# Window attention into a gated feed-forward layer on one core: masks in six steps, one inversion for both heads, an untied exponential, and earlier weights

## The chip, the core and the metric

The kernel runs on one core of a Trainium2 chip. The core has five engines that work through queues of their own, each in order: TensorE (PE; its weight loads are shown apart as PEld), VectorE (DVE), ScalarE (ACT), GpSimd (POOL) and SyncE (SP), which here only issues transfers; 16 DMA engines carry those out. The metric is the device time of one execution in microseconds (us). The kernel before takes 1011.78 us, the median of three runs (1010.85 to 1012.56).

## The reference

Eight batches of eight heads (head size 64) attend over 576 positions, each position to itself and the 63 before it. The result, 4608 tokens of 512 numbers, goes through a gated feed-forward layer. Everything is in 32-bit floats in and out.

```python
scores = scale * np.matmul(q, k.transpose(0, 1, 3, 2))
mask = (rel >= 0) & (rel < window)
scores = np.where(mask, scores, -1000000000.0)
scores = scores - np.max(scores, axis=-1, keepdims=True)
attn = np.exp(scores)
attn = attn / (np.sum(attn, axis=-1, keepdims=True) + 1e-09)
out = np.matmul(attn, v)
...
gate = 1.0 / (1.0 + np.exp(-(x @ w_gate)))
val = x @ w_val
return (gate * val @ w_out).astype(np.float32)
```

## The kernel before

**Tiling.** The 4608 tokens are 12 tiles of 384 (t, in an order of their own). The eight heads are four pairs (p = 0 to 3), so a tile has four units of attention, written (t,p). In a unit the 384 tokens are six blocks of 64, and a block attends to 128 keys (its own and the block before). The hidden layer's 1536 columns are 12 blocks of 128 (j); each j has three weight matrices, m = 0 (gate), 1 (value) and 2 (output). The number of a weight piece is i = 3j + m, so i = 3 and 4 are gate and value of the second block, i = 2 and 5 the output weights of the first and second.

**One unit of attention.** TensorE makes the scores of both heads (`s0`, `s1`, L208). VectorE adds the mask, scales, and takes the row minimum of the negated scores (L230, three per head). ScalarE takes the exponentials (L239, three per head); the row sums of head 0 come with them, those of head 1 of tiles 0 and 1 from a VectorE reduction (L248). VectorE adds 1e-9 and inverts (L249, L250), and GpSimd multiplies the rows by the inverses (L252). TensorE transposes (`pp`, L283), ScalarE copies the result out (`pT`, L288), TensorE multiplies by v (`oo`, L312), and ScalarE and VectorE split the result into a high and a low part (`x`, L318 and L319).

**The front.** All eight units of tiles 0 and 1 come first. Each step has a due time in a list of events: unit n = 4t + p has its scores at A0 + 3.6n, its softmax, transposes and products at fixed distances behind. The events are sorted by due time; that is the order in which the code issues them. TensorE keeps that order. On the other engines a scheduler orders the instructions by its own estimate, within the dependencies and the bindings that the code gives with `tc.issue_after(x)`: an instruction issued within it comes behind x. In the front the exponentials of unit n are bound behind the transposed copies of unit n - 2.

**The weights.** Each weight piece arrives as 64-bit words (`raw`, six buffers) and is turned into 32-bit floats: ScalarE makes two conversions (`w32` L111, `raw` L112; three `w32` buffers), VectorE three bit operations (`zz` L120, then L122, L124), ScalarE the rounded high part (L145) and VectorE the low part (L146). For m < 2 the float form is stored (`w32d`, L139), and parts of the split form too (`wd`, L447), for the tiles that come later. A `w32` buffer is free again when its store has landed. `conv_a`, `conv_b` and `conv_c` are bound behind marks: in the front those of i = 3 behind the split of unit (1,2), those of i = 2, 4 and 5 behind that of (1,3).

**Tiles 0 and 1, then pairs of tiles.** The hidden blocks of tiles 0 and 1 follow: for each j the gate product (`ph0`, 12 matmuls of 384 columns, L342), the value product (`ph1`), and, one block behind, the output product (`y`, nine matmuls of 512 columns, L407). The `ph` products go round three PSUM banks. The gate's sigmoid (`g`, L363) is ScalarE's, and needs another function table than the exponentials (an ACT_TABLE_LOAD at each change). From tile 2 on the tiles go in pairs with seven products in place of eight (`pr`, L537), and the attention of the next pair is spread between them.

**The masks.** Three 128x128 masks are made before all else: one for inner blocks, two for the first block of a sequence, one for each head. GpSimd sets each to zero and cuts it with selections on 64 rows.

Of the code, what the change and the prediction touch: the masks (L58 to L72), `softmax`, `exponentials`, `normalize` and `stage_n` (L212 to L276), the table of due times (L608 to L612) and the marks of the conversions (L732 to L748).

## Time and profile before

| what | us |
|---|---|
| median of three runs | 1011.78 |
| the profiled execution, its own time | 1013.32 |
| its span, first to last instruction | 1011.5 |
| TensorE busy in the span | 981.8 (97%) |
| VectorE busy | 675.8 (67%) |
| ScalarE busy | 527.2 (52%) |
| GpSimd busy | 236.1 (23%) |

A share is a mean over the whole span. The front and the stretch of the conversions, the first 100 us or so, load the engines otherwise than the rest. A TensorE that is shown busy may be waiting inside a matmul, since ends of matmuls are modelled; the number of matmuls in a stretch says more. The granted clock is given as a share of 2.4 GHz.

### The profile page before, as it was taken

What the parts mean: (1) busy time and instruction counts of PE and PEld (TensorE: products, weight loads), DVE (VectorE), ACT (ScalarE), POOL (GpSimd) and SP (SyncE); (2) the same over time, 40 slices, a digit from 0 to 9 for tenths busy, and PEclk for the clock granted to TensorE, in tenths of its full rate; (3) what the DMA queues carried; (4) which work ended last, traced back from release to release, by engine and by line L of the source; (5) the groups of instructions that cost most, each with busy time, mean ns of one, the idle gap of its engine ahead of it and who ended that gap; (6) DMA issues with size and microseconds to landing.
All of it is one profiled execution on the core that took longest, in us unless ns stands there. A gap on an engine that the chain in (4) does not pass through costs nothing.

```text
span 1011.5 us, 19901 instructions
## 1 busy us (share of the span) xinstructions
PE 981.8 (97%) x6984; PEld 884.0 (87%) x6984; DVE 675.8 (67%) x1846; ACT 527.2 (52%) x1465; POOL 236.1 (23%) x251
## 2 busy tenths in 40 slices
PE   5899999998999999999999999999999999999998
PEld 4798998887899978999988999988999998999996
DVE  6789889757887874766675766675666677344542
ACT  7878886744654644545554654554555454211122
POOL 5200117254540030212131221213211124010100
PEclk9999999999999999999999999999999999999999
DMA  9899988899997624767652776760776662466500
GB/s 299 297 348 367 342 288 278 277 333 342 320 324 267 216 85 152 232 220 221 202 172 70 240 234 200 222 204 32 228 232 219 207 192 74 146 219 204 192 32 32
DMA packets 115924, 221.52 MB, mean 219 GB/s; under 512 B 9456, under 2 KB 61936, under 8 KB 115824
## 3 DMA queue, kind: packets, MB, share of 16 engines
q1 hardware_dynamic: 115824, 220.24, 65.9%
q8 instruction: 56, 0.92, 0.4%
q14 instruction: 44, 0.36, 0.1%
HBM read 178.52 MB, written 41.68 MB: 218 GB/s over the span
## 4 chain that ended last, share of the span: by engine, by line
PE 73%; DVE 7%; ACT 7%; DMA 6%; issue 3%; POOL 1%; SPq 0%; DVEq 0%; ACTq 0%; POOLq 0%
PE pr L537 36%; PE y L407 24%; PE ph L342 6%; ACT p L239 3%; PE pp L283 2%; PE s L208 2%; DMA wd<-w 2%; DMA wd<-ws 2%; ACT g L352 1%; ACT e L351 1%; PE oo L312 1%; PE s L312 1%; DMA wt<-wd 1%; DVE u L543 1%; DVE p L230 1%
## 5 line engine op out<-in xcount | busy, mean ns | idle before, releaser
L537 PE MATMUL pr<-x_T,wt 128*128 128x384 f32 x1440 | 284.6, 339 | 4.7 <-DVE u L543 3.6
L537 PEld LDWEIGHTS pr<-x_T,wt 128*128 128x128 f32 x1440 | 252.6, 188 | 20.1 <-DVE u L543 11.2
L407 PE MATMUL y<-w,hh 128*128 128x512 f32 x804 | 250.2, 392 | 0.0
L537 PE MATMUL pr<-x_B,wt 128*128 128x384 f32 x1080 | 222.2, 342 | 4.7 <-ACT xf L267 4.0
L537 PEld LDWEIGHTS pr<-x_B,wt 128*128 128x128 f32 x1080 | 188.7, 189 | 15.6 <-ACT xf L267 4.3
L407 PEld LDWEIGHTS y<-w,hh 128*128 128x128 f32 x804 | 148.3, 188 | 21.3 <-ACT hh L372 1.3
L543 DVE TENSOR_TENSOR u<-pr,p 128x384 f32<-128x384 f32 x120 | 66.6, 555 | 143.3 <-PE pr L537 143.0
L407 PE MATMUL y<-w,hl 128*128 128x512 f32 x402 | 158.6, 394 | 0.5 <-DVE hl L376 0.4
L252 POOL TENSOR_TENSOR p<-p,rs 128x384 f32<-128x384 f32 x76 | 65.0, 860 | 278.2 <-DVE rs L250 227.5
L239 ACT ACTIVATE p<-p,mn 128x128 f32<-128x128 f32 x288 | 111.1, 394 | 23.6 <-DVE mn L230 22.7
L376 POOL TENSOR_TENSOR hl<-h,hh 128x384 fp32r<-128x384 f32 x48 | 49.8, 1038 | 296.2 <-DVE hh L374 296.2
L342 PE MATMUL ph<-x,w 128*128 128x384 f32 x576 | 109.2, 343 | 1.8 <-DVE w L146 1.3
L342 PEld LDWEIGHTS ph<-x,w 128*128 128x128 f32 x576 | 100.9, 190 | 5.4 <-DVE w L146 1.6
L407 PEld LDWEIGHTS y<-w,hl 128*128 128x128 f32 x402 | 75.3, 187 | 19.3 <-DVE hl L376 3.1
L230 DVE CUSTOM_DVE_ANT_0 p<-s,m 128x128 f32<-128x128 f32 x288 | 66.4, 285 | 15.7 <-PE s L208 8.5
L543 DVE TENSOR_TENSOR c<-pr,u 128x384 f32<-128x384 f32 x120 | 66.6, 555 | 7.8 <-ACT g L568 3.3
L376 DVE TENSOR_TENSOR hl<-hb,hh 128x384 fp32r<-128x384 f32 x60 | 39.1, 663 | 40.9 <-ACT hh L372 40.5
L351 ACT ACTIVATE e<-c 128x384 f32<-128x384 f32 x72 | 37.4, 522 | 52.6 <-DVE c L543 51.6
L548 ACT COPY p<-pr 128x384 f32<-128x384 f32 x60 | 28.2, 470 | 70.4 <-PE pr L537 69.8
L288 ACT COPY pT<-pp 128x384 f32<-128x384 f32 x96 | 41.2, 481 | 41.6 <-PE pp L283 41.6
L356 DVE SCALAR_TENSOR_TENSOR g<-g,e 128x384 f32<-128x384 f32 x96 | 55.2, 589 | 5.7 <-ACT e L353 5.6
L354 DVE TENSOR_SCALAR g<-g 128x384 int32<-128x384 int32 x96 | 40.2, 425 | 25.9 <-ACT g L352 25.9
(84 smaller groups left out, 1238.7 us busy)
## 6 DMA issues: line engine op xcount, KB each, us to landing
wt<-wd SPq DMA_DIRECT2D x210, 512.0 KB, 4.2
v<-in_vN_dram SPq DMA_DIRECT2D x48, 384.0 KB, 4.9
wd<-ws SPq DMA_DIRECT2D x48, 256.0 KB, 5.3
k<-in_kT_dram SPq DMA_DIRECT2D x48, 224.0 KB, 5.0
q<-in_qT_dram SPq DMA_DIRECT2D x48, 192.0 KB, 4.7
wd<-w SPq DMA_DIRECT2D x36, 256.0 KB, 6.0
out_dram<-yo SPq DMA_DIRECT2D x33, 256.0 KB, 2.0
raw<-in_moe_w_gate_dram SPq DMA_DIRECT2D x12, 512.0 KB, 5.9
```

What stands on the lines that cost most here:

```text
L230: nc.vector.tensor_tensor_reduce(out=pt[:, u, :], in0=sc[:, u, :], in1=masks[key], op0=ALU.add, op1=ALU.min, scale=-SCALE, scalar=3.0e38, ...
L239: exp = nc.scalar.activation(pt[:, u, :], pt[:, u, :], AF.Exp, bias=mn[:, u:u + 1], scale=-1.0, **sums)
L252: eng.tensor_mul(out=pt, in0=pt, in1=rs.unsqueeze(2).broadcast_to([P, UP, P]))
L288: cp = nc.scalar.copy(pT, pp)
L342: pe(nc.tensor.matmul(ph, l, r, start=i == 0, stop=i == len(prs) - 1))
L351: nc.scalar.activation(e, ph, AF.Relu, scale=-1.0)
L354: nc.vector.tensor_scalar(out=g.bitcast(I32), in0=g.bitcast(I32), scalar1=0x7FFFFFFF, scalar2=None, op0=ALU.bitwise_and)
L356: nc.vector.scalar_tensor_tensor(out=g, in0=g, scalar=1.0, in1=e, op0=ALU.add, op1=ALU.mult)
L376: return eng.tensor_sub(out=h_lo, in0=h32, in1=h_hi.bitcast(F32))
L407: pe(nc.tensor.matmul(yb[y], l, r, start=first and n == 0, stop=last and n == 2))
L537: pe(nc.tensor.matmul(ps, l, r, start=new and i == 0, stop=i == len(prs) - 1, skip_group_check=not new))
L543: nc.vector.tensor_add(out=o, in0=ps, in1=a)
```

## The change

It has four parts.

1. The inner mask is set to zero by VectorE and cut by GpSimd in four selections. The two other masks are VectorE copies of it, each cut once more on 64 rows. This stands ahead of the identity matrix; before, the identity and three memsets came first or between, and fourteen selections made the masks.
2. The row sums of both heads of a unit lie in one tile (`rs`, 128x6). One addition and one inversion serve both, and the two multiplications follow. `normalize` now takes a whole unit, in all 12 tiles.
3. The exponentials of unit (1,3) are not bound behind the transposed copies of (1,1). The due times of the transposes and products of units (1,2) and (1,3) move forward: 9.2 and 10.4 for n = 6 in place of 10.6 and 12.2, 7.3 in place of 8.4 for the transposes of n = 7.
4. The conversions of i = 3 follow the split of unit (1,1), those of i = 4 that of (1,2).

```diff
+    masks = {key: const.tile([P, P], F32, name=f"m_{key[0]}{key[1]}") for key in ((0, 0), (1, 0), (0, 1))}
+    band = masks[0, 0]
+    nc.vector.memset(band, 0.0)
+    for h in range(2):
+        rows = band[h * BLK:(h + 1) * BLK]
...
+    for h, key in enumerate(((1, 0), (0, 1))):
+        nc.vector.tensor_copy(out=masks[key], in_=band)
+        rows = masks[key][h * BLK:(h + 1) * BLK]
+        nc.gpsimd.affine_select(out=rows, in_=rows, pattern=[[1, P]], compare_op=ALU.is_ge,
+                                fill=NEG, base=-BLK, channel_multiplier=0)
     ident = const.tile([P, P], F32, name="ident")
     make_identity(nc, ident)
...
             exponentials(t, p, h, sc[h])
-            normalize(t, p, h)
+        normalize(t, p)
...
-        rs = sm.tile([P, UP], F32, name=f"rs{h}_{t}_{p}", tag="rs")
+        if h == 0:
+            rs_of[(t, p)] = sm.tile([P, 2, UP], F32, name=f"rs_{t}_{p}", tag="rs")
+        rs = rs_of[(t, p)][:, h, :]
...
-                if NP * t + p - 2 in marks["pT"]:
+                if NP * t + p - 2 in marks["pT"] and (t, p) != (1, NP - 1):
...
-    def normalize(t, p, h):
-        pt, rs = st[(t, p, h)]
-        if t < 2 and h:
-            nc.vector.reduce_sum(out=rs, in_=pt, axis=mybir.AxisListType.X)
+    def normalize(t, p):
+        rs = rs_of.pop((t, p))
+        if t < 2:
+            nc.vector.reduce_sum(out=rs[:, 1, :], in_=st[(t, p, 1)], axis=mybir.AxisListType.X)
         nc.vector.tensor_scalar_add(out=rs, in0=rs, scalar1=1e-9)
         nc.vector.reciprocal(out=rs, in_=rs)
         eng = nc.vector if t == 3 and p % 2 or t // 2 == 2 else nc.gpsimd
-        eng.tensor_mul(out=pt, in0=pt, in1=rs.unsqueeze(2).broadcast_to([P, UP, P]))
-        st[(t, p, h)] = pt
+        for h in range(2):
+            pt = st[(t, p, h)]
+            eng.tensor_mul(out=pt, in0=pt, in1=rs[:, h, :].unsqueeze(2).broadcast_to([P, UP, P]))
...
-                        (0, 3.5 if n > 1 else 0, 10.6 - n // 7 * 2.2, 12.2)):
+                        (0, 3.5 if n > 1 else 0, {6: 9.2, 7: 7.3}.get(n, 10.6), {6: 10.4}.get(n, 12.2))):
...
-                early = {3: ("1_2",), 2: ("1_3",), 4: ("1_3",), 5: ("1_3",)}.get(a[0], (key,))
+                early = {3: ("1_1",), 4: ("1_2",), 2: ("1_3",), 5: ("1_3",)}.get(a[0], (key,))
```

How the instructions stand now is shown at three places. The first is GpSimd's queue from the start of the program to its first multiplication, before (`m_00`, `m_10` and `m_01` are the masks).

```order
masks.py:197 MEMSET ident_81 128x128
L61 MEMSET m_00_86 128x128
masks.py:199 ISA
masks.py:199 AFFINE_SELECT ident_81<-ident_81 128x128
L64 AFFINE_SELECT m_00_86<-m_00_86 64x128 x2
L61 MEMSET m_10_100 128x128
L66 AFFINE_SELECT m_00_86<-m_00_86 64x128
L61 MEMSET m_01_117 128x128
...
L66 AFFINE_SELECT m_01_117<-m_01_117 64x128 x2
L69 AFFINE_SELECT m_10_100<-m_10_100 64x128
L69 AFFINE_SELECT m_01_117<-m_01_117 64x128
L252 TENSOR_TENSOR p0_0_0_266<-p0_0_0_266,rs0_0_0_268 128x384
```

And the same place in the changed kernel.

```order
L61 ISA
L61 AFFINE_SELECT m_00_81<-m_00_81 64x128 x2
masks.py:197 MEMSET ident_105 128x128
L63 AFFINE_SELECT m_00_81<-m_00_81 64x128 x2
masks.py:199 AFFINE_SELECT ident_105<-ident_105 128x128
L68 AFFINE_SELECT m_10_82<-m_10_82 64x128
L68 AFFINE_SELECT m_01_83<-m_01_83 64x128
L256 TENSOR_TENSOR p0_0_0_242<-p0_0_0_242,rs_0_0_244 128x384
L256 TENSOR_TENSOR p1_0_0_251<-p1_0_0_251,rs_0_0_244 128x384
```

Fourteen selections on masks have become six, and the three memsets have gone; the scheduler has put the identity's two instructions between them. The two multiplications of a unit now take one `rs` tile.

The second place is ScalarE's queue at the end of the front, before (`p0_1_3` is head 0 of unit (1,3), `x_1_1` the split of unit (1,1), `g_0_0` the first gate of tile 0, `w32_0_1` the conversion of i = 3).

```order
L239 ACTIVATE p1_1_2_668<-p1_1_2_668,mn1_1_2_669 128x128 x3
L318 CAST x_1_0_708<-oo_1_0_695 128x384
L288 COPY pT0_1_1_715<-pp0_1_1_711 128x384
L288 COPY pT1_1_1_721<-pp1_1_1_717 128x384
L239 ACTIVATE p0_1_3_723,rs0_1_3_725<-p0_1_3_723,mn0_1_3_724 128x128 x3
L239 ACTIVATE p1_1_3_735<-p1_1_3_735,mn1_1_3_736 128x128 x3
L318 CAST x_1_1_761<-oo_1_1_748 128x384
L363 ACT_TABLE_LOAD
L363 ACTIVATE g_0_0_777<-ph0_0_0_764 128x384
...
L318 CAST x_1_2_835<-oo_1_2_822 128x384
L111 ACTIVATE w32_0_1_838<-raw_0_1_330 128x512
```

And in the changed kernel.

```order
L241 ACTIVATE p1_1_2_623<-p1_1_2_623,mn1_1_2_624 128x128 x3
L241 ACTIVATE p0_1_3_678,rs_1_3_680<-p0_1_3_678,mn0_1_3_679 128x128 x3
L241 ACTIVATE p1_1_3_687<-p1_1_3_687,mn1_1_3_688 128x128 x3
L317 CAST x_1_0_663<-oo_1_0_650 128x384
L287 COPY pT0_1_1_670<-pp0_1_1_666 128x384
L287 COPY pT1_1_1_676<-pp1_1_1_672 128x384
L317 CAST x_1_1_713<-oo_1_1_700 128x384
L111 ACTIVATE w32_0_1_790<-raw_0_1_300 128x512
...
L145 CAST w0_1_797<-w32_0_1_790 128x2x256
L362 ACT_TABLE_LOAD
L362 ACTIVATE g_0_0_741<-ph0_0_0_728 128x384
```

The exponentials of (1,3) have gone ahead of the split of (1,0), and the whole conversion of the second block's gate weights stands ahead of the table load. On TensorE the transposes of (1,2) have gone ahead of the first gate product, the products of (1,2) and the transposes of (1,3) ahead of the first value product.

The third place is ScalarE's queue around `g_1_0`, the first gate of tile 1, before (`w32_0_2` and `w32_1_2` are conversions of the third block).

```order
L363 ACTIVATE g_1_0_880<-ph0_1_0_867 128x384
L145 CAST w0_1_845<-w32_0_1_838 128x2x256
L145 CAST w1_1_940<-w32_1_1_907 128x2x256
L112 ACTIVATE raw_0_2_882<-raw_0_2_882 128x512
L112 ACTIVATE raw_1_2_884<-raw_1_2_884 128x512
L145 CAST w2_0_950<-w32_2_0_912 128x512
L111 ACTIVATE w32_0_2_972<-raw_0_2_882 128x512
L111 ACTIVATE w32_1_2_977<-raw_1_2_884 128x512
```

And in the changed kernel.

```order
L317 CAST x_1_3_816<-oo_1_3_803 128x384
L111 ACTIVATE w32_2_0_864<-raw_2_0_389 128x512
L112 ACTIVATE raw_2_0_389<-raw_2_0_389 128x512
L111 ACTIVATE w32_0_2_924<-raw_0_2_834 128x512
L112 ACTIVATE raw_2_1_862<-raw_2_1_862 128x512
L111 ACTIVATE w32_1_2_929<-raw_1_2_836 128x512
L362 ACTIVATE g_1_0_832<-ph0_1_0_819 128x384
L145 CAST w2_0_902<-w32_2_0_864 128x512
```

`g_1_0` stood ahead of the third block's conversions and stands behind two of them now. From the tenth block on the queues of all engines are alike but for the normalization.

## Rows read from the trace of the kernel before

**Rows 1.** The page: the span, the busy time of TensorE, and the shares of the chain that ended last.

```profile
span 1011.5 us, 19901 instructions
PE 981.8 (97%) x6984; PEld 884.0 (87%) x6984; DVE 675.8 (67%) x1846; ACT 527.2 (52%) x1465; POOL 236.1 (23%) x251
PE 73%; DVE 7%; ACT 7%; DMA 6%; issue 3%; POOL 1%; SPq 0%; DVEq 0%; ACTq 0%; POOLq 0%
```

**Rows 2.** The windows view: stretch in us, its length, busy time (and instructions) of PE, PEld, DVE, ACT and POOL, the granted clock, the DMA engines' busy share, and GB/s.

```profile
25.00:30.00 5.00, 2.79 (x38) 1.77 (x32) 4.96 (x34) 5.00 (x20) 2.10 (x3) 1.00 1.05 388
40.00:45.00 5.00, 4.84 (x69) 4.25 (x67) 3.67 (x8) 4.20 (x10) 0.00 (x0) 1.00 0.41 129
45.00:50.00 5.00, 3.41 (x17) 2.77 (x17) 4.94 (x10) 4.71 (x10) 0.00 (x0) 1.00 0.92 250
50.00:55.00 5.00, 5.00 (x20) 5.00 (x21) 3.52 (x8) 3.13 (x6) 0.00 (x0) 0.66 0.86 216
80.00:100.00 20.00, 18.71 (x154) 16.53 (x154) 18.98 (x48) 17.09 (x37) 2.26 (x2) 1.00 1.03 376
100.00:120.00 20.00, 20.00 (x157) 18.70 (x150) 17.08 (x57) 16.56 (x40) 1.82 (x2) 1.00 0.95 346
```

**Rows 3.** The timeline of the start: start in us, length, engine, line and operation, and in brackets the idle time before it and what ended that. The first scores, GpSimd's last mask selections, the first mask addition, the first exponential.

```profile
3.91 1.56 PE L208 MATMUL s<-k,q 64*64 64x128 f32 x24 [3.91 <-DMA k<-in_kT_dram]
1.35 0.64 POOL L64 TENSOR_SCALAR_AFFINE_SELECT m<-m 64x128 f32<-64x128 f32 x2
5.97 0.64 POOL L69 TENSOR_SCALAR_AFFINE_SELECT m<-m 64x128 f32<-64x128 f32 x2
6.29 0.29 DVE L230 CUSTOM_DVE_ANT_0 p<-s,m 128x128 f32<-128x128 f32 x1 [5.43 <-POOL m L69]
6.62 0.40 ACT L239 ACTIVATE p<-p,mn 128x128 f32<-128x128 f32 x1 [4.40 <-DVE mn L230]
```

**Rows 4.** The timeline of VectorE and GpSimd around 26 to 29 us: head 1's inversion of unit (1,0), an addition that runs beside a multiplication, and then GpSimd's multiplications of (1,0) head 1 and (1,1) head 0.

```profile
26.74 0.17 DVE L250 RECIPROCAL rs<-rs 128x3 f32<-128x3 f32 x1
27.27 0.66 DVE L249 TENSOR_SCALAR rs<-rs 128x3 f32<-128x3 f32 x1
27.08 0.82 POOL L252 TENSOR_TENSOR p<-p,rs 128x384 f32<-128x384 f32 x1 [1.63 <-DVE rs L250]
28.28 0.83 POOL L252 TENSOR_TENSOR p<-p,rs 128x384 f32<-128x384 f32 x1 [0.38 <-DVE rs L250]
```

**Rows 5.** The timeline of ScalarE from the copies of (1,0) to the gate's table load, and the first conversions and high parts of the second block.

```profile
28.23 0.86 ACT L288 COPY pT<-pp 128x384 f32<-128x384 f32 x2
30.14 0.99 ACT L239 ACTIVATE p<-p,mn 128x128 f32<-128x128 f32 x3
32.96 0.48 ACT L318 CAST x<-oo 128x384 fp32r<-128x384 f32 x1 [1.83 <-PE oo L312]
33.84 0.86 ACT L288 COPY pT<-pp 128x384 f32<-128x384 f32 x2 [0.40 <-PE pp L283]
34.58 0.41 ACT L239 ACTIVATE p<-p,mn 128x128 f32<-128x128 f32 x1
36.63 0.46 ACT L318 CAST x<-oo 128x384 fp32r<-128x384 f32 x1
38.04 1.28 ACT L363 ACT_TABLE_LOAD   x1 [0.95 <-PE ph L342]
39.34 0.49 ACT L363 ACTIVATE g<-ph 128x384 f32<-128x384 f32 x1
42.63 0.67 ACT L111 ACTIVATE w<-raw 128x512 f32<-128x512 f32 x1
43.20 0.67 ACT L112 ACTIVATE raw<-raw 128x512 int32<-128x512 uint32 x1
47.29 0.64 ACT L145 CAST w<-w 128x512 fp32r<-128x512 f32 x1
```

**Rows 6.** The timeline of TensorE from the first gate product to the first output product.

```profile
35.59 2.37 PE L342 MATMUL ph<-x,w 128*128 128x384 f32 x12
45.01 2.70 PE L342 MATMUL ph<-x,w 128*128 128x384 f32 x14 [0.17 <-DVE x L319]
47.98 0.62 PE L342 MATMUL ph<-x,w 128*128 128x384 f32 x2 [0.27 <-ACT w L145]
49.91 5.66 PE L342 MATMUL ph<-x,w 128*128 128x384 f32 x22 [1.31 <-DVE w L146]
55.41 0.63 PE L407 MATMUL y<-w,hh 128*128 128x512 f32 x2
```

**Rows 7.** The timeline again: a conversion's steps on VectorE (`zz`, L122, L124), a ScalarE conversion that waits for a store, and one scores product later on. Then, from the view of the transfers between 40 and 100 us, the stores of the float weights: issues, KB each, us to landing.

```profile
43.33 0.43 DVE L120 TENSOR_SCALAR zz<-w 128x512 int32<-128x512 int32 x1
43.80 0.69 DVE L122 SCALAR_TENSOR_TENSOR w<-w,zz 128x512 int32<-128x512 int32 x1
44.87 0.68 DVE L124 CUSTOM_DVE_ANT_0 w<-raw,w 128x1024 uint16<-128x1024 uint16 x1
52.91 1.24 ACT L111 ACTIVATE w<-raw 128x512 f32<-128x512 f32 x2 [1.87 <-DMA w32d<-w]
80.95 0.88 PE L208 MATMUL s<-k,q 64*64 64x128 f32 x22 [1.07 <-ACT xf L300]
...
w32d<-w SPq DMA_DIRECT2D x11, 256.0 KB, 5.3
```

More of the change, by code (lines that the diff above doesn't have):

```diff
@@ L53, in attn_ffn @@
     ps_a = ctx.enter_context(tc.tile_pool(name="ps_a", bufs=2, space=PSUM))
+    masks = {key: const.tile([P, P], F32, name=f"m_{key[0]}{key[1]}") for key in ((0, 0), (1, 0), (0, 1))}
[4 more added lines that the diff above has]
+        nc.gpsimd.affine_select(out=rows, in_=rows, pattern=[[1, P]], compare_op=ALU.is_ge,
+                                fill=NEG, base=-1, channel_multiplier=-1)
+        nc.gpsimd.affine_select(out=rows, in_=rows, pattern=[[-1, P]], compare_op=ALU.is_ge,
+                                fill=NEG, base=BLK, channel_multiplier=1)
+    for h, key in enumerate(((1, 0), (0, 1))):
+        nc.vector.tensor_copy(out=masks[key], in_=band)
+        rows = masks[key][h * BLK:(h + 1) * BLK]
+        nc.gpsimd.affine_select(out=rows, in_=rows, pattern=[[1, P]], compare_op=ALU.is_ge,
+                                fill=NEG, base=-BLK, channel_multiplier=0)
     ident = const.tile([P, P], F32, name="ident")
     make_identity(nc, ident)
-    masks = {}
-    for key in ((0, 0), (1, 0), (0, 1)):
-        m = const.tile([P, P], F32, name=f"m_{key[0]}{key[1]}")
-        nc.gpsimd.memset(m, 0.0)
-        for h in range(2):
-            rows = slice(h * BLK, (h + 1) * BLK)
-            nc.gpsimd.affine_select(out=m[rows], in_=m[rows], pattern=[[1, P]], compare_op=ALU.is_ge,
-                                    fill=NEG, base=-1, channel_multiplier=-1)
-            nc.gpsimd.affine_select(out=m[rows], in_=m[rows], pattern=[[-1, P]], compare_op=ALU.is_ge,
-                                    fill=NEG, base=BLK, channel_multiplier=1)
-            if key[h]:
-                nc.gpsimd.affine_select(out=m[rows], in_=m[rows], pattern=[[1, P]], compare_op=ALU.is_ge,
-                                        fill=NEG, base=-BLK, channel_multiplier=0)
-        masks[key] = m
     warm = const.tile([P, 1], F32, name="warm")
@@ L153, in attn_ffn @@
     xs, xf = {}, {}
-    ld, vts, st, kk, sc_of = {}, {}, {}, {}, {}
+    ld, vts, st, kk, sc_of, rs_of = {}, {}, {}, {}, {}, {}
     def load_qk(t, p):
@@ L242, in exponentials @@
                 chain.append(exp.ins)
-        st[(t, p, h)] = pt, rs
-    def normalize(t, p, h):
-        pt, rs = st[(t, p, h)]
-        if t < 2 and h:
-            nc.vector.reduce_sum(out=rs, in_=pt, axis=mybir.AxisListType.X)
+        st[(t, p, h)] = pt
+    def normalize(t, p):
+        rs = rs_of.pop((t, p))
+        if t < 2:
+            nc.vector.reduce_sum(out=rs[:, 1, :], in_=st[(t, p, 1)], axis=mybir.AxisListType.X)
         nc.vector.tensor_scalar_add(out=rs, in0=rs, scalar1=1e-9)
@@ L272, in stage_s @@
         exponentials(t, p, 1, sc[1])
-    def stage_n(t, p):
-        for h in range(2):
-            normalize(t, p, h)
     def stage_b(t, p):
@@ L596, in attn_ffn @@
     APT = (0.9, 0.8, 0.9, 1.5, 0)
-    stages = (stage_a, stage_b, stage_c, stage_s, stage_n)
+    stages = (stage_a, stage_b, stage_c, stage_s, normalize)
     LOAD_AHEAD = 8
```

## The prediction

> **What bounds the kernel now.** I read the page first. TensorE is busy 97% of the span and has 73% of the chain that ended last [rows 1], so the other engines count only where TensorE waits. The windows view says where that is [rows 2]. From 100 us on a stretch of 20 is full: 157 matmuls in 20.00 us busy. Before that there are holes. Between 25 and 30 us TensorE is busy 2.79 of 5 while ScalarE has 5.00 and VectorE 4.96: the front belongs to these two. Between 45 and 50 it runs 17 instructions where 5 us have room for 27 matmuls of the size seen below. Between 50 and 55 its granted clock is 0.66 on the mean, so it ran part of that stretch at 1.2 GHz instead of 2.4.
>
> The timelines then give the reasons. At the start the first mask addition waits for GpSimd's last masks, not for the scores [rows 3]. Before 45 us ScalarE waits 1.83 and 0.40 us for TensorE, and the exponentials of the last unit stand behind those waits [rows 5]. At 47.98 TensorE waits 0.27 us for the second block's weights, at 49.91 again 1.31, and the 22 matmuls from there take 5.50 us to the first output product [rows 6]. I look for the gain there, since behind it TensorE goes on with little idle time.
>
> **The masks.** The last selection ends at 5.97 + 0.64 = 6.61, the first addition starts at 6.29; the scores that it also needs end at 3.91 + 1.56 = 5.47 [rows 3]. A selection costs 0.32. Six of them and two instructions for the identity, at that price each, are 2.6 us from about 0.9, so the masks are there by 4 us; VectorE's memset and two copies run beside them. The addition then waits for the scores alone and starts near 5.55: 0.7 us earlier. It can't be more, because the scores wait for k from the DMA.
>
> **One inversion for both heads.** Removed per unit: one addition and one inversion, about 0.2 us of VectorE. Something else goes too: the addition of head 0 ran beside GpSimd's multiplication of the unit before and took 0.66 instead of the 0.17 of a neighbouring inversion; it ends as GpSimd does (27.08 + 0.82) [rows 4]. In the new order the addition stands behind the reduction and some mask additions, where GpSimd is done. Against that stands a longer path: both multiplications wait for the one inversion, where head 0's ran ahead of it. Behind the inversion of (1,0) at 26.74, GpSimd ended 27.90 and the copies began at 28.23 [rows 4, 5]; now 0.83 comes on top. The start's 0.7 and some 0.4 of VectorE's go into paying for that. I take 0.25 us earlier for the exponentials of (1,2), which end at 30.75 instead of 31.0. The bounds: 0.8 earlier if the second multiplication hides behind ScalarE's other work, 0.5 later if VectorE saves nothing. In the later tiles the 48 units lose as many instructions, but TensorE is the bound there: nothing.
>
> **The untied exponentials.** Those of (1,3) need the mask additions of (1,3), which stand behind a reduction: 0.75 us behind 30.75, so 31.5, in place of 34.58 [rows 5]. They take 2.05 (34.58 to 36.63). From here ScalarE is nearly full, and I add its queue in the new order, by start-to-start times [rows 5]: the split of (1,0) 0.36 and the copies of (1,1) 0.74 end at 34.65, about where the copies ended before. The product of (1,1) takes TensorE 0.9; its split ends at 35.95 (before 37.0). The 3 us won are filled with other work, not yet a gain.
>
> **The second block's weights.** The two conversions of i = 3 come now (0.57 and 0.56, to 37.1) instead of at 42.63. Then the copies of (1,2), to 37.8. The high part, which came at 47.29, waits for three VectorE steps of 0.35, 0.6 and 0.6 [rows 7]: 38.1 to 38.6. The table load 1.28 and the gate 0.40 end at 40.3, some 0.6 later than before [rows 5]. Split of (1,2) 0.36, the conversions of i = 4 1.13, the copies of (1,3) 0.74: 42.5. The high part of i = 4 (waiting for VectorE) 43.4, two `raw` 1.12, the split of (1,3) 0.36: 44.9, and its low part on VectorE 0.47: 45.35. TensorE's 14 matmuls need that low part; they started at 45.01 [rows 6]. So up to here the kernel is 0.35 us *later*: the conversions were moved ahead of the split, and ScalarE is the queue that everything stands in.
>
> But the weights are there by 44.2. The 14 matmuls end near 47.85, and the 24 of block 1 follow at once. Twelve take 2.17 at full clock (35.59: 2.37 less the last one's overlap of 0.2), so 24 take 4.35: the first output product starts at 52.2, in place of 55.41. Gain 3.2 us. About 1.6 of it are the two waits, 1.5 the clock (22 matmuls at 0.181 are 4.0, not 5.5), and the rest small.
>
> That assumes that the clock doesn't fall. Before it fell TensorE had run two matmuls between 47.7 and 49.91 [rows 6]. In the new order I see one idle stretch of 0.9 us ahead of the products of (1,3), with work on either side. If the clock falls all the same, 1.5 us are lost again.
>
> **The sum.** The page's span is 1011.5 in an execution of 1013.32, which is 1.54 above the median of 1011.78. 1013.32 - 3.2 = 1010.1 in that execution, and 1011.78 - 3.2 = **1008.6** against the median. This takes it that 55 to 100 us, where the conversions keep VectorE (18.98 of 20) and the DMA engines (share 1.03) full [rows 2], moves forward as a whole. I think so, since the DMA engines have a hole to fill: 129 and 250 GB/s between 40 and 50 us against 376 later [rows 2], together some 1.9 MB or 5 us of transfers, and the changed order issues the second block's stores and the fourth block's loads into it.
>
> One rule speaks against moving the table load into a full stretch. In the trace the load takes 1.28 us and the gate starts 0.02 behind it [rows 5]; ahead of it stand 0.95 us idle which the view puts to TensorE. The Trainium skill's page "ScalarE: Activation LUTs", section "What ACT_TABLE_LOAD costs", counts a drain of about 1.38 us to each switch on top of the load. By that rule the forecast would be an estimate of 1010.0 us. The trace disagrees behind the load; ahead of it the idle time leaves room for a drain that the wait hides.
>
> **The rivals.**
> *The later losses go too (0.10).* TensorE loses 1.07 us at 80.95 to a copy on ScalarE [rows 7] and between 80 and 100 is busy 18.71 of 20. With the conversions further ahead these 1.3 go, and the front could keep 0.8 instead of 0.25 and 0.35 lost: 3.2 + 1.3 + 0.9 = 5.4, or 1006.4. For it: the hole at the DMA. Against it: the order of copies and conversions on ScalarE around 80 us is no better than it was.
> *Half is given back (0.20).* With VectorE and DMA full from 60 to 100 us, the conversions might not come forward by more than what the hole took in. If half of its 5 us is filled, or the clock falls once more, 1.2 to 1.7 of the gain stay: 1010.3. Against it: in these 40 us TensorE hardly waits, so they were only just the bound.
> *The gates stand behind the stores: slower (0.10).* `g_1_0` is now behind the third block's two conversions, which take the buffers of the second block's and so wait for their stores. A store lands 5.3 us after its issue, and ScalarE did wait 1.87 us for one at 52.91 [rows 7], with the gate behind it but two blocks of products ahead. TensorE stops if `g_1_0` ends later than the third product after its own starts in the same bank, near 50.0. Its queue gives 49.9, with the store issued at 43.6. That is close. If it comes 2 us late, and the same happens in each of the blocks 1 to 3, TensorE loses 5.7 us and gains 3.2: 1014.3.
> *The load costs more in the full stretch (0.05).* If the 0.95 us idle ahead of the load belong to it, the queue above is 0.95 longer, and so is the split of (1,3): 1009.5. The row gives no more.
>
> **How the numbers follow.** The forecast has 0.55, with a range of its own of 1007.4 to 1009.8. 0.2% is 2.0 us, about what a measurement of this kernel can tell, so "faster" begins below 1009.8. Faster: 0.54 of the forecast, 0.10 of the first rival, 0.03 of the last, 0.67 together. Within: the second rival and what is left, 0.23. Slower: 0.10. The range runs from the first rival's side to the given-back case with some margin: 1006.0 to 1011.8.
>
> **What would show it right or wrong.** The first mask addition at 5.5 to 5.6 us and bound by the scores. The exponentials of (1,3) at 31 to 32. The load of the sigmoid's table about 39, behind a conversion. The split of (1,3) no earlier than before, 44 to 45.5. No wait of TensorE for weights near 48, clock 1.00 from 45 to 55, and the first output product at 51.5 to 53. At 100 us the same matmuls 3 us earlier. Wrong would be: a wait for a gate between 48 and 62 us, a granted clock of 0.5 there, or a first output product at 52 whose lead is gone at 100.

## The result and the profile after

The changed kernel takes 1019.51 us, the median of seven runs (1014.17 to 1022.27), where the kernel before, measured beside it, takes 1012.72 (1010.85 to 1016.79). The ratio is 1.0055 with a 95% interval from 1.0036 to 1.0075: it is **slower** by about half a per cent. The prediction said 1008.6 and faster.

The page of the changed kernel, in an execution of 1019.14 us (its span, the busy times, and the chain that ended last by engine):

```profile
span 1017.4 us, 19764 instructions
PE 984.9 (97%) x6984; PEld 886.9 (87%) x6984; DVE 660.5 (65%) x1753; ACT 527.4 (52%) x1465; POOL 233.9 (23%) x240
PE 70%; ACT 9%; DVE 8%; DMA 6%; issue 3%; POOL 1%; SPq 0%; DVEq 0%; ACTq 0%; POOLq 0%
```

Beside [rows 1] VectorE has 15.3 us less to do (675.8 to 660.5), yet the span is 5.9 longer, and ScalarE and VectorE have more of the chain. TensorE's own 6984 matmuls take 3.1 us longer (984.9 for 981.8), and it is idle 2.8 longer. So it waits more, and runs more of its work at the lower clock.

**The front, in this trace, comes earlier.** The timeline of the changed kernel's front: first VectorE's first mask addition, then ScalarE from the exponentials of (1,3) to the split of x(1,3).

```profile
5.63 0.29 DVE L232 CUSTOM_DVE_ANT_0 p<-s,m 128x128 f32<-128x128 f32 x1 [2.48 <-PE s L208]
...
29.09 0.40 ACT L241 ACTIVATE p<-p,mn 128x128 f32<-128x128 f32 x1
...
32.05 0.40 ACT L241 ACTIVATE p<-p,mn 128x128 f32<-128x128 f32 x1 [0.83 <-DVE mn L232]
...
39.39 0.62 ACT L145 CAST w<-w 128x512 fp32r<-128x512 f32 x1 [0.73 <-DVE w L124]
40.03 1.28 ACT L362 ACT_TABLE_LOAD   x1
41.32 0.49 ACT L362 ACTIVATE g<-ph 128x384 f32<-128x384 f32 x1
...
44.78 0.62 ACT L145 CAST w<-w 128x512 fp32r<-128x512 f32 x1 [0.73 <-DVE w L124]
45.31 1.25 ACT L112 ACTIVATE raw<-raw 128x512 int32<-128x512 uint32 x2
46.45 0.46 ACT L317 CAST x<-oo 128x384 fp32r<-128x384 f32 x1
```

The mask addition now waits for the scores instead of the masks (5.63, was 6.29 in [rows 3]); the exponentials of (1,3) start at 32.05 instead of 34.58. TensorE's timeline answers to [rows 6]:

```profile
46.97 0.44 PE L341 MATMUL ph<-x,w 128*128 128x384 f32 x1 [0.18 <-ACT x L317]
47.56 6.86 PE L341 MATMUL ph<-x,w 128*128 128x384 f32 x38 [0.15 <-DVE x L318]
54.26 0.63 PE L406 MATMUL y<-w,hh 128*128 128x512 f32 x2
```

No wait for weights is left, 38 matmuls run at one go, and the first output product starts at 54.26, which is 1.15 us earlier than before. The windows view has the clock at 1.00 from 40 to 55 us and the transfers up (columns as in [rows 2]):

```profile
40.00:45.00 5.00, 4.16 (x45) 3.63 (x43) 3.31 (x6) 4.24 (x9) 0.00 (x0) 1.00 0.97 300
45.00:50.00 5.00, 4.67 (x25) 4.10 (x25) 4.65 (x10) 4.78 (x10) 0.00 (x0) 1.00 1.00 313
50.00:55.00 5.00, 5.00 (x30) 4.87 (x29) 4.92 (x11) 3.36 (x8) 0.00 (x0) 1.00 0.99 342
```

**The lead is lost behind it.** First the windows view of before from 60 us on, then of the changed kernel:

```profile
60.00:80.00 20.00, 19.88 (x149) 18.33 (x138) 18.53 (x49) 16.55 (x37) 1.92 (x2) 1.00 1.02 363
```

```profile
60.00:80.00 20.00, 18.26 (x116) 17.31 (x116) 17.33 (x46) 17.65 (x38) 1.74 (x2) 0.95 0.91 316
80.00:90.00 10.00, 10.00 (x71) 9.20 (x70) 7.61 (x28) 8.51 (x22) 0.50 (x1) 0.93 1.04 355
90.00:100.00 10.00, 8.08 (x60) 7.07 (x59) 9.76 (x18) 5.84 (x13) 1.82 (x2) 0.92 0.95 329
```

In the first 20 us TensorE is busy 18.26 where it was 19.88, and from 60 to 100 us the granted clock is 0.92 to 0.95 on the mean where it was 1.00. The wait view says what TensorE waits for: TensorE's waits between 40 and 245 us (producer, us in total, times, longest), before and changed.

```profile
PE pr L537 <- ACT xf L267: 4.0, 1, 4.0
...
PE oo L312 <- ACT pT L288: 0.2, 1, 0.2
```

```profile
PE oo L311 <- ACT pT L287: 5.7, 7, 1.7
PE s L208 <- ACT xf L299: 1.9, 2, 1.7
```

`pT` are ScalarE's copies of the transposed probabilities of the tiles from the third on, whose attention runs between the hidden blocks of tiles 0 and 1; `xf` are its copies of their attention's output. The 4.0 of before stands near 242 us; the changed kernel has the same wait with 2.0, but behind 245 us, so it isn't in its list. How the first such wait comes about is seen on ScalarE between 72 and 78 us, before and then changed:

```profile
74.04 0.46 ACT L363 ACTIVATE g<-ph 128x384 f32<-128x384 f32 x1
74.86 0.68 ACT L111 ACTIVATE w<-raw 128x512 f32<-128x512 f32 x1 [0.35 <-DVE w L146]
75.44 0.83 ACT L288 COPY pT<-pp 128x384 f32<-128x384 f32 x2
77.32 0.62 ACT L145 CAST w<-w 128x512 fp32r<-128x512 f32 x1 [1.05 <-DVE w L124]
```

```profile
73.19 0.48 ACT L362 ACTIVATE g<-ph 128x384 f32<-128x384 f32 x1
75.55 0.62 ACT L145 CAST w<-w 128x512 fp32r<-128x512 f32 x1 [1.89 <-DVE w L124]
76.08 0.85 ACT L287 COPY pT<-pp 128x384 f32<-128x384 f32 x2
```

The cast is the high part of `w0_4` (the fifth block's gate weights), which waits for VectorE. Before, the copies of (2,0) stood ahead of it; now they stand behind it and wait with it, though the gate ahead of both is 0.85 us earlier. The change's text doesn't touch these lines. The scheduler lists each engine's work by a model of when it is ready, and with the front's work moved forward its listing of all later conversions came out differently, down to block 10. TensorE pays twice here. First before, then changed:

```profile
77.17 2.35 PE L342 MATMUL ph<-x,w 128*128 128x384 f32 x12
```

```profile
72.58 2.34 PE L341 MATMUL ph<-x,w 128*128 128x384 f32 x12
76.60 1.29 PE L311 MATMUL oo<-pT,v 128*64 128x64 f32 x24 [1.69 <-ACT pT L287]
77.83 3.92 PE L341 MATMUL ph<-x,w 128*128 128x384 f32 x12
```

It idles 1.69 us, and the next twelve matmuls take 3.92 us where the same twelve took 2.35 before, at the lower clock (1.2 GHz) for a part: the granted clock is 0.66 on the mean from 77 to 82 us. The same happens at 98 us behind waits of 1.31 and 0.61 (clock 0.66 from 98 to 103), and at 180 behind one of 1.71 for `xf` (0.57 from 180 to 184). The clock doesn't fall each time, as e8 below shows.

To see where the time went over the whole span I take the start of the same matmul in both traces (TensorE's order is the same from the first output product on). Given is how much later it starts than in before; the later columns belong to the experiments below. Each is one execution.

| matmul at (before, us) | changed | again (e8) | e5 | e6 | e13 | e15 |
|---|---|---|---|---|---|---|
| 62.5 | -1.15 | -0.11 | -0.04 | +0.13 | -0.16 | -1.59 |
| 81.0 | +0.74 | +3.09 | -1.85 | +4.91 | -1.72 | -1.68 |
| 99.3 | +3.54 | +4.38 | +1.13 | +7.72 | -2.24 | -1.17 |
| 173.6 | +6.08 | +5.38 | +1.02 | +9.72 | -0.78 | -1.50 |
| 369.9 | +7.91 | +8.60 | +3.02 | +13.18 | +0.53 | +1.10 |
| 1007.6 | +5.85 | +6.58 | +1.44 | +10.81 | -1.52 | -0.99 |

Most of the loss lies between 62 and 174 us: 7.2 us in the first trace, 5.5 in the second. From 174 to 370 us each of these kernels, all with the joined inversion, loses 1.3 to 3.5 us more, e15 too, which is not slower in the end; and from 370 us to the end each wins back 1.6 to 2.4.

One trace doesn't tell what the new front is worth. The first output product starts between 54.26 and 55.48 in the six traces with the whole changed front (the changed kernel, e3, e5, e8, e9, e13), and between 52.31 and 55.54 in the five whose front has only the first two parts of the change (e4, e6, e10, e11, e15). So it isn't shown that the third and fourth part bring it forward.

### The profile page after: what moved, and what is told of

It is laid out like the page before. It is cut to its first block, busy times and chain, and to the rows that moved or that the text cites. A ratio compares the mean times of both kernels' runs of the same rounds, so it can differ in the third digit from the quotient of the medians.

```text
span 1017.4 us, 19764 instructions
## 1 busy us (share of the span) xinstructions
PE 984.9 (97%) x6984; PEld 886.9 (87%) x6984; DVE 660.5 (65%) x1753; ACT 527.4 (52%) x1465; POOL 233.9 (23%) x240
## 4 chain that ended last, share of the span: by engine, by line
PE 70%; ACT 9%; DVE 8%; DMA 6%; issue 3%; POOL 1%; SPq 0%; DVEq 0%; ACTq 0%; POOLq 0%
PE pr L536 37%; PE y L406 23%; PE ph L341 4%; ACT p L241 3%; DMA wd<-ws 2%; PE pp L282 2%; PE s L208 2%; PE s L311 1%; DMA wd<-w 1%; DVE w L124 1%; DVE w L122 1%; ACT raw L112 1%; ACT g L351 1%; PE oo L311 1%; DVE x_T L516 1%
## 5 line engine op out<-in xcount | busy, mean ns | idle before, releaser
L375 POOL TENSOR_TENSOR hl<-h,hh 128x384 fp32r<-128x384 f32 x48 | 49.9, 1039 | 283.8 <-DVE hh L373 283.8
L341 PEld LDWEIGHTS ph<-x,w 128*128 128x128 f32 x576 | 103.6, 195 | 3.0 <-issue 1.1
L375 DVE TENSOR_TENSOR hl<-hb,hh 128x384 fp32r<-128x384 f32 x60 | 39.1, 663 | 40.9 <-ACT hh L371 40.5
L355 DVE SCALAR_TENSOR_TENSOR g<-g,e 128x384 f32<-128x384 f32 x96 | 57.8, 615 | 4.5 <-ACT e L352 4.3
L371 ACT CAST hh<-hb 128x384 fp32r<-128x384 f32 x60 | 30.0, 512 | 51.5 <-PE y L406 51.5
```

The source lines that it names most:

```text
L341: pe(nc.tensor.matmul(ph, l, r, start=i == 0, stop=i == len(prs) - 1))
L355: nc.vector.scalar_tensor_tensor(out=g, in0=g, scalar=1.0, in1=e, op0=ALU.add, op1=ALU.mult)
L371: nc.scalar.copy(h_hi, h32)
L375: return eng.tensor_sub(out=h_lo, in0=h32, in1=h_hi.bitcast(F32))
```

## The experiments

The first theory was: the order of ScalarE in the conversion stretch costs, in that the copies of the transposed probabilities stand behind conversions that wait for VectorE. The rivals: the joined inversion costs (A), an earlier front costs whatever stands behind it (B). Ratios are to the kernel before on the same chip, with 95% intervals.

**e1, e2, e4, e7: the parts apart.** e1 is the changed kernel with the marks of before, e2 the kernel before with the new marks alone. The edit of e1 is shown; that of e2 is its reverse in the other kernel:

```diff
-                early = {3: ("1_1",), 4: ("1_2",), 2: ("1_3",), 5: ("1_3",)}.get(a[0], (key,))
+                early = {3: ("1_2",), 2: ("1_3",), 4: ("1_3",), 5: ("1_3",)}.get(a[0], (key,))
```

e4 is e1 without the untied exponentials and their due times too (so the masks and the inversion alone), e7 the changed kernel without the untied exponentials and due times:

```diff
-                if NP * t + p - 2 in marks["pT"] and (t, p) != (1, NP - 1):
+                if NP * t + p - 2 in marks["pT"]:
...
-                        (0, 3.5 if n > 1 else 0, {6: 9.2, 7: 7.3}.get(n, 10.6), {6: 10.4}.get(n, 12.2))):
+                        (0, 3.5 if n > 1 else 0, 10.6 - n // 7 * 2.2, 12.2)):
```

> The changed kernel without its last part: the second block's weights follow the marks of before, all else stays changed. Theory (the order): the earlier conversions pull all later ones forward in ScalarE's order, so that the copies of the transposed probabilities of tiles 2 and 3 stand behind conversion steps that wait for VectorE; in this kernel's order both copies of (2,0) stand ahead of w0_4's high part again and both copies of (2,2) ahead of w32_0_6. Then most of the loss goes: 1011 to 1015 us against 1012.7 of before and 1019.5 of the changed kernel, TensorE waits under 2.5 us for transposed probabilities between 40 and 400 us (5.7 in the changed kernel, 0.2 before), and no 1.2 GHz stretch at 78 or 99. Rival A (the joined inversion, with GpSimd's two multiplications in one go, is what costs): it stays at 1018 to 1020. Rival B (an earlier front collides with other work wherever the order stands): the first output product moves back to 55 or later and the time falls to 1012 to 1013, with the waits at 76 and 96 there or not in step with the order.

> The kernel before with the last part of the change alone: w_gate's second block follows x(1,1), w_val's x(1,2). Theory (the order): its ScalarE order has w32_2_3 ahead of the copies of (2,0), but these still ahead of w0_4's high part, and w32_0_6 ahead of both copies of (2,2), so a part of the loss shows: 1014 to 1018 us, with TensorE waiting 1.5 to 4 us for transposed probabilities between 40 and 400 us. Rival A (the joined inversion costs): 1011 to 1013, no such waits above 0.5 us. Rival B (an earlier front collides): the front is not earlier here by more than 0.5 us, so 1012 to 1013.

> The first two parts of the change alone: the masks in 6 steps and the inversion of both heads' sums as one; exponentials, due times and marks of the weights as before. ScalarE's order is that of before but for two places near 90 us. Theory (the order): 1011.5 to 1013 us, with TensorE's waits as before (4 us for xf near 242, 0.2 for transposed probabilities). Rival A (the joined inversion costs): 1016 to 1020, with waits for GpSimd's products or for what follows them. Rival B (an earlier front collides): as the front gains 0 to 0.5 us here, 1012 to 1013.5.

> The changed kernel without its third part: exponentials of (1,3) tied and due times as before, but the second block's weights follow the marks of the change. With e4 (neither the third nor the fourth part, 1012.5), e1 (the third, 1015.3) and the changed kernel (both, 1019.5) it makes a table of two by two. Theory (the order, to which both parts add moves): 1014 to 1016.5 us, that is 2 to 4 above e4, so that the parts add up. Rival C (only the two together cost, as the load of the gate's table and the second block then come at once): 1012 to 1013.5.

Measured: e1 1015.32 us, ratio 1.0019 (1.0000 to 1.0039); e2 1015.37, 1.0026 (1.0008 to 1.0044); e4 1012.46, 0.9985 (0.9961 to 1.0009); e7 1013.84, 0.9996 (0.9979 to 1.0013). The times of e2 and e4 came out as the order theory has it, that of e1 0.3 above its range, that of e7 between its range and rival C's. e1's trace goes against its expectation: both copies of (2,0) stand ahead of `w0_4`, yet TensorE waits 0.87 and 0.60 us for them, since a conversion that stands in front of them waits for VectorE, and the next twelve matmuls take 3.91 us. ScalarE in e1:

```profile
76.41 0.67 ACT L111 ACTIVATE w<-raw 128x512 f32<-128x512 f32 x1 [1.26 <-DVE w L146]
```

e2 doesn't tell the order from rival B, because its front is not as late as I had assumed: the first output product starts 1.86 us earlier than before in its trace. Rival A falls: e4 has the joined inversion in all 48 units and is not slower. On top of e4 the third part costs 0.34%, the fourth 0.11% (within the noise), both 0.70%. That both together cost more than their sum lies within the intervals, so it isn't shown.

**e3: only the copies first.** In the changed kernel the conversions queue behind the latest copies of a tile from the third on:

```diff
+            else:
+                marks["copied"] = (cp.ins,)
...
+                early += ("copied",)
                 for ins in [i for nm in early for i in marks.get(nm, ())]:
```

> The changed kernel with one rule more: the steps of a conversion that stand later in the program than the copies of the transposed probabilities of a tile from the third on are queued behind them on ScalarE. Theory (the order): the waits of TensorE for these copies go back under 1 us between 40 and 400 us, its clock keeps 2.4 GHz at 78 and 99, the lead of 1.15 us at the first output product is kept, and the time is 1007 to 1012 us, below before. Rival A (the joined inversion): 1018 to 1020, since nothing of it is changed. Rival B (an earlier front collides): the time stays above 1015 with other waits in place of these.

Measured: 1019.65 us, ratio 1.0068 (1.0047 to 1.0089). The waits went as expected, the time didn't. TensorE's waits between 40 and 245 us, and then ScalarE at the longer of the two gate waits:

```profile
PE ph L343 <- ACT g L364: 3.4, 2, 2.0
PE oo L313 <- ACT pT L287: 1.3, 2, 0.8
```

```profile
164.08 0.62 ACT L145 CAST w<-w 128x512 fp32r<-128x512 f32 x1 [0.88 <-DVE w L124]
164.72 1.28 ACT L364 ACT_TABLE_LOAD   x1
166.01 0.49 ACT L364 ACTIVATE g<-ph 128x384 f32<-128x384 f32 x1
```

Waits for `pT` fell from 5.7 to 1.3, the lead was 1.11 us at 96; then gates, which stand behind the delayed conversions and a table load, made TensorE wait 3.4. That is what rival B foretold: no gain, and other waits in place of these. So the first theory was too narrow. The next two runs ask whether the listing as a whole, or the earlier front, decides.

**e5 and e6: the listings exchanged.** Instead of single rules, ScalarE's and VectorE's instructions behind the front were written down in another kernel's order and tied in a row (e5: the changed kernel in the order of e4; e6: e4 in the order of the changed kernel):

```diff
+        for item in listed.split():
+            name, k = item.split(":")
+            ins = found[name][int(k)]
+            if last is not None:
+                tc.add_manual_dep(ins, last.name, mybir.DependencyInfo(
+                    mybir.DependencyClass.NoSync, mybir.DependencyReason.DATA), reason="in_order")
+            last = ins
```

> The changed kernel whole, but ScalarE's and VectorE's instructions from the second block's VectorE work and the third block's first conversion on (115 and 166 of them, to the last step of w2_8) are written down in the order in which the kernel with the first two parts alone (e4) has them, which on ScalarE is that of before but for two places. The front is that of the change. Theory (the order of blocks 2 to 8, taken as a whole and not the copies of the transposed probabilities alone, costs): the front's gain of about 1 us stays and the losses behind go: 1008 to 1013 us. Rival B (the earlier front itself costs, whatever stands behind it): 1017 to 1020 us as the changed kernel, with waits of TensorE in other places.

> The reverse: the kernel with the first two parts alone (e4, 1012.5 us), its exponentials, due times and marks as before, but ScalarE's and VectorE's instructions behind the second block's (121 and 170 of them, to w2_8) in the changed kernel's order. Theory (the order costs): the time rises by most of the loss, 1016 to 1020 us, with TensorE's waits for transposed probabilities at 3 us or more between 40 and 250 us. Rival B (the earlier front costs): 1011 to 1014 us, since the front is that of e4.

Measured: e6 1020.68 us, ratio 1.0073 (1.0049 to 1.0097, six runs). The old front with the changed listing loses 8.2 us against e4 (0.88% by the two ratios, as they ran on different chips), and its trace has the same waits: ScalarE's copies of (2,0) behind the cast at 79.76, and TensorE's wait.

```profile
79.76 0.62 ACT L146 CAST w<-w 128x512 fp32r<-128x512 f32 x1 [1.36 <-DVE w L125]
```

```profile
80.81 1.35 PE L312 MATMUL oo<-pT,v 128*64 128x64 f32 x24 [2.90 <-ACT pT L288]
```

So the listing is enough for the loss, with the old front too. e5: 1015.96, ratio 1.0034 (1.0013 to 1.0055), above its range and below rival B's. The changed kernel on the same chip (e8) has 1.0053 (1.0031 to 1.0075); the intervals overlap, so it isn't shown that the old listing gives anything back here. Whether tying VectorE's instructions in a row costs by itself was not tried; ScalarE's, tied in a kernel's own order with six steps moved besides, cost nothing that shows (e10, e14 below). Where e5's trace loses is seen at 90 us, TensorE and ScalarE:

```profile
90.77 3.46 PE L342 MATMUL ph<-x,w 128*128 128x384 f32 x10 [2.26 <-ACT g L363]
```

```profile
83.96 0.67 ACT L112 ACTIVATE w<-raw 128x512 f32<-128x512 f32 x1 [2.12 <-DMA w32d<-w]
84.64 1.28 ACT L242 ACT_TABLE_LOAD   x1
...
88.93 1.28 ACT L363 ACT_TABLE_LOAD   x1
90.23 0.49 ACT L363 ACTIVATE g<-ph 128x384 f32<-128x384 f32 x1
```

TensorE is 1.86 us ahead of before when it gets there; the gate that it needs starts at 90.23, where before had it at 89.88. ScalarE had waited 2.12 for a store of float weights. In this trace the stretch keeps a pace of its own, and a TensorE that comes earlier waits in it.

**e8: the changed kernel again.**

> The changed kernel once more, for a second trace and for its time beside the other kernels on one chip. Theory (the order, which is the same in every execution): TensorE's waits for transposed probabilities near 76 and near 96 us are there again within 0.5 us each, and the median is 1018 to 1021 us. Rival D (the losses of the first trace are those of one execution, from the clock or the DMA): other waits in other places, and a median nearer to 1014.

Measured: 1019.50 us, ratio 1.0053 (1.0031 to 1.0075). In its trace the cast of `w0_4` waits 1.89 again, TensorE 2.87 for the copies behind it, 6.3 for all `pT` between 40 and 245 (5.7 in the first). The size of the single wait was off by more than the 0.5 expected, its place was the same. The front's lead was 0.11 here, not 1.15. Behind the copies of (2,2) TensorE waits 1.30 and 0.61, as in the first trace, but the twelve matmuls that follow run at full clock:

```profile
101.34 2.38 PE L341 MATMUL ph<-x,w 128*128 128x384 f32 x12
```

And the cast of `w0_4` on ScalarE:

```profile
77.94 0.62 ACT L145 CAST w<-w 128x512 fp32r<-128x512 f32 x1 [1.89 <-DVE w L124]
```

**e9, e10, e13, e14: less for VectorE.** If the listing costs because VectorE is late, taking work from it must help. The low parts of `w_out`'s blocks 2 to 7 go to GpSimd, in the changed kernel (e9), in e4 (e10), in e5 (e13) and in e7 (e14), with ScalarE's listing held in the last three (VectorE's listing, which e5 holds too, is free in e13):

```diff
-            cp = split(w32, hi, lo, nc.vector)
+            cp = split(w32, hi, lo, nc.gpsimd if 2 <= j < 8 else nc.vector)
```

> The changed kernel, with the low parts of w_out's blocks 2 to 7 (six subtractions, about 0.7 us each on VectorE) made by GpSimd instead, which does little before 140 us. ScalarE's order stays the changed kernel's up to five single moves. Theory (no slack: in the conversion stretch the order costs because VectorE, busy 17 to 20 us of each 20, is late, so whatever stands behind a conversion waits with it): the wait of w0_4's high part near 76 us (1.89 in both traces of the changed kernel) falls by some 0.7 us or more, TensorE's waits for transposed probabilities fall from 4.4 to 4.8 to under 3.5, and the time to 1013 to 1017.5. Rival E (the order alone, whatever VectorE does): these waits stay and the time is 1018.5 to 1021. Rival F (GpSimd's work slows VectorE's): VectorE's conversion steps become longer than 0.71 us and the time is above 1020.

> The first two parts alone (e4), with the same six subtractions on GpSimd, and ScalarE's 115 instructions of the conversion stretch written down in e4's order, so that they don't move. Theory (no slack): TensorE's waits between 40 and 245 us become fewer, and the time is 1008 to 1011.5, below e4's 1012.5. Rival E (the order alone): as e4, 1012 to 1013.5. Rival F (GpSimd's work slows VectorE's): above 1013.5.

> e5 (the changed front, ScalarE's order behind it as in e4) with the six low parts of w_out's blocks 2 to 7 on GpSimd as in e9 and e10. Theory (the stretch from 60 to 245 us keeps its own pace because VectorE is late in it, so an earlier TensorE only waits there): with VectorE relieved the lead holds, and the ratio to before falls from 1.0034 to 0.998 to 1.001 (1011 to 1014 us). Rival H (the pace is that of ScalarE's queue itself, with its table loads and exponentials, or of the transfers): the wait of some 2 us for the gate near 90 stays and the ratio is 1.002 to 1.004.

> The parts 1, 2 and 4 (e7, ratio 0.9996) with the six low parts of w_out's blocks 2 to 7 on GpSimd and ScalarE's 116 instructions of the conversion stretch written down in e7's own order. Theory (VectorE's pace): its waits for transposed probabilities (2.8 us between 40 and 110) become shorter as in e9, and the ratio falls to 0.996 to 0.999. Rival H (ScalarE's queue or the transfers): 0.999 to 1.001 as e7.

Measured: e9 1016.37 us, ratio 1.0025 (1.0004 to 1.0046), half of the loss by the medians, with an interval that overlaps e8's. The cast of `w0_4` waits 0.53 less (0.7 was expected). TensorE's waits for `pT` between 40 and 245 are shorter in sum, though the longest, 1.9, is still the one behind this cast:

```profile
76.99 0.62 ACT L145 CAST w<-w 128x512 fp32r<-128x512 f32 x1 [1.36 <-DVE w L124]
```

```profile
PE oo L311 <- ACT pT L287: 3.4, 4, 1.9
```

But VectorE did not get less to do. The page of e9:

```profile
PE 981.2 (97%) x6984; PEld 883.6 (87%) x6984; DVE 660.6 (65%) x1747; ACT 527.6 (52%) x1465; POOL 242.9 (24%) x246
```

Six instructions are gone, and the busy time is 660.6 where it was 660.5: other instructions take longer, between 55 and 150 us the step at L124 724 ns on the mean for 684, a subtraction of 128x384 (L375) 675 for 595. In e13 the busy time is 662.8 where e5 has 659.1.

e13 1013.07, ratio 0.9991 (0.9971 to 1.0012), as expected, and clear of e5's. The gate that came late in e5 comes in time (ScalarE), and TensorE goes through (28 matmuls at one go):

```profile
86.84 1.28 ACT L363 ACT_TABLE_LOAD   x1
88.13 0.49 ACT L363 ACTIVATE g<-ph 128x384 f32<-128x384 f32 x1
```

```profile
85.71 5.32 PE L342 MATMUL ph<-x,w 128*128 128x384 f32 x28
```

e10 1014.00, 0.9996 (0.9977 to 1.0016): a miss, with the old front and the old listing the move brought no gain that can be measured. e14 1013.47, 0.9988 (0.9964 to 1.0013), can't be told from e7. So with ScalarE's old listing and the six steps on GpSimd the changed front is no longer slower, and not faster than the old one either. That VectorE's load is the reason is not shown: its busy time didn't fall, and against e5 its listing became free as well.

**e11: the rule of e3, for `pT` and `xf`, in e4.**

> The first two parts alone (e4), with the rule that the steps of a conversion that stand later in the program than the copies of a tile's transposed probabilities and of its output (from the third tile on) queue behind these on ScalarE. Theory (the order decides): TensorE's waits for pT and xf below 245 us (0.6, 0.5, 0.6 and 2.0 in e4) fall under 1 in sum, and the time is 1009 to 1012. As in e3 it may go the other way, since then the conversions are late and a gate or the weights wait: 1013 to 1016, with TensorE waiting for gates behind conversions.

Measured: 1015.75 us, ratio 1.0021 (1.0001 to 1.0040). It went the other way, as in e3: TensorE's waits of scores for `xf` fell from 2.6 to 0.2 us, those for `pT` rose from 1.0 to 1.8, and the transposes waited 1.8 between 40 and 245 us for VectorE's and GpSimd's multiplications. A rule against one wait moves others.

**e12: only the due times back.**

```diff
-                        (0, 3.5 if n > 1 else 0, {6: 9.2, 7: 7.3}.get(n, 10.6), {6: 10.4}.get(n, 12.2))):
+                        (0, 3.5 if n > 1 else 0, 10.6 - n // 7 * 2.2, 12.2)):
```

> The changed kernel with the due times of the transposes and output products of (1,2) and (1,3) as before; exponentials of (1,3) untied, masks, inversion and weights' marks as changed. In its ScalarE order both copies of (2,0) stand ahead of w0_4's high part again and those of (2,2) behind w32_0_6 and w32_1_6. Theory (the order costs, and the due times are what moved the copies): 1013 to 1016 us, some 4 under the changed kernel, without a wait of TensorE over 1 us for w0_4's sake at 76. Rival G (the untied exponentials cost, wherever the copies stand): 1017 to 1020.

Measured: 1014.68 us beside 1011.11 of before, ratio 1.0029 (1.0011 to 1.0047): by the ratio, half of the loss goes with the due times, as the order theory has it and not rival G; the interval overlaps e8's. In its trace the copies of (2,0) stand ahead of `w0_4` and TensorE has no wait for them; at 96 it waits 1.21 for those of (2,2).

**e15: the masks and the inversion once more.**

> e4 once more, as its ratio of 0.9985 had an interval from 0.9961 to 1.0009. If the first two parts gain what they gain in the front and on VectorE (about 0.7 us at the masks, 15 us of VectorE's time), the ratio is again 0.9975 to 0.9995; if the first result was chance, 0.9995 to 1.001.

Measured: 1012.30 us beside 1014.14, ratio 0.9973 (0.9954 to 0.9992). With e4's 0.9985 (whose interval includes 1) the mean of the two is 0.998: the first two parts alone are a version that beats both kernels, the one before by about 0.2%.

## Why the prediction was wrong

*The masks.* Right: predicted 0.7 us earlier, measured 0.66 at the first addition.

*One inversion.* The front pays for GpSimd's two multiplications in a row about as reckoned: the exponentials of (1,2) start at 29.09 instead of 28.97, 0.1 later where I had 0.25 earlier, inside the bounds. "TensorE is the bound there: nothing" came out about right for the later tiles, but as a sum of two things: from 174 to 370 us the changed kernel loses 1.83 us (6.08 to 7.91), and from there to the end it gains 2.06 (7.91 to 5.85), e1, e4 and e15 1.9, 1.9 and 2.1. In that last stretch, from 400 us on, before has 1.5 us of waits for `u`, which VectorE makes from the pair products, and the changed kernel none.

*The untied exponentials.* They start at 32.05, predicted 31.5: ScalarE waits 0.83 us for the mask addition on VectorE.

*The weights.* The mechanism was right: no wait for weights, full clock from 45 to 55, 38 matmuls at one go. The size was off: 54.26 instead of 52.2, a gain of 1.15 instead of 3.2. The term that was mis-sized is ScalarE's queue. The exponentials came 0.55 late; the sum leaves 0.3 and 0.4 us for the two high parts to wait for VectorE, and both waited 0.73; what remains of the 2 us lies in small pieces of the queue. The second trace had 55.30, so even the 1.15 is the better of two, and by the spread of the traces above it can be chance.

*The table load.* The rival that gives it 0.95 us more falls, and so does, for this switch, the rule of the Trainium skill's page "ScalarE: Activation LUTs", section "What ACT_TABLE_LOAD costs". In [rows 5] the idle time ahead of the load left room for a drain; here the cast ahead ends at 39.39 + 0.62 = 40.01, the load starts at 40.03 and the gate at 41.32. Neither side shows a drain. The trace of before had it already, one load further on, where nothing is idle ahead of it (62.48 + 0.61 = 63.09):

```profile
62.48 0.61 ACT L145 CAST w<-w 128x512 fp32r<-128x512 f32 x1
63.11 1.28 ACT L239 ACT_TABLE_LOAD   x1
```

*The step that failed* is in the sum: that 55 to 100 us "moves forward as a whole". I gave as reason that the DMA engines had a hole to fill. They filled it: 300 and 313 GB/s between 40 and 50 us, where before had 129 and 250 [rows 2]. The stretch didn't follow. TensorE's wait at 76 us is for copies on ScalarE that stand behind a conversion which waits for VectorE, in a new listing, and between 62 and 174 us the lead of 1.15 became a lag of 6.08. e6 shows that the new listing does this with the old front too. I followed the new listing where the change was, between 28 and 50 us, and called that around 80 us "no better than it was"; it was worse, with the copies of (2,0) and (2,2) behind conversions. The rival with the right sign named gates behind stores, but `g_1_0`, which ran at 49.97 us, did not stop TensorE. Its kind was right (something that TensorE needs stands behind a conversion), its place was one tile further on.

*The clock.* The forecast took it that it doesn't fall. Between 45 and 55 us it didn't; behind some of the new waits it did. Over the 12 runs of e8 the mean granted clock is 0.9924 where before's 29 runs have 0.9944. At the lower level (1.2 GHz of 2.4) half of the work isn't done, so 0.001 of mean clock is about 1 us of span. By this estimate 2 of the 5.3 us between the means are clock; the rest would be idle time, and the traces' 2.8 and 3.1 us more of idle TensorE agree with it.

What stays open: which engine sets the pace of the stretch (in the kernel before ScalarE waits there, between 50 and 90 us, 5.2 us for transfers and 2.5 for VectorE); what of e5's loss comes from a listing that was made for another front, what from tying VectorE's instructions and what from the stretch's pace as such; and why the due times and the marks together cost more than apart, if they do.

## What to carry to other kernels

A change of order ahead of a stretch with several nearly full engines changes the scheduler's listing in that stretch. Compare the two listings to its end, on each engine, and ask of each instruction that TensorE waits for what now stands ahead of it and whom that waits for. A few us gained in front of such a stretch count only if the engine that paces it gets them too; and ties for one wait move the next one. When work is moved to another engine, compare the busy time of the engine that gave it up: here it didn't fall. The two parts that only removed work were worth keeping alone.

## What had not been expected

One order of instructions gives times over several us: e8's twelve runs lie between 1012.97 and 1023.53, and the places behind the front where the clock falls differ between the kernel's two traces (near 78, 98 and 180 us in the first, near 80 and 247 in the second). A single trace tells which wait comes back, but not its size: the wait for the copies of (2,0) was 1.69 in one and 2.87 in the other. Nor is a trace one of a middling run: those of e4 and e6 are of their slowest, those of e2, e3, e9 and e10 of their fastest.
